# An early exp-table load, and the first pair's half step as one full-height product

## The chip, the cores and the metric

The kernel runs on one core of a Trainium2 chip. The metric is the device time of one execution in microseconds (us), lower is better. Several executions were timed; the median is given with the lowest and the highest. One further execution was taken with the hardware profiler, and its trace is what the views below are read from. The core has five engines with instruction queues of their own: TensorE (PE in the profile, with its weight loads as PEld), VectorE (DVE), ScalarE (ACT), GpSimd (POOL) and SyncE (SP), which here only issues DMAs. A small q behind a name (SPq) is the engine's sequencer.

## The reference

Attention of 8 batches with 12 heads, 448 positions and head size 64, whose softmax has one more term in its denominator; the result, laid out as 3584 tokens of 768, goes through two dense layers with Mish between them.

```python
scores = scale * np.matmul(q, k.transpose(0, 1, 3, 2))
m = np.max(scores, axis=-1, keepdims=True)
e = np.exp(scores - m)
attn = e / (np.sum(e, axis=-1, keepdims=True) + np.exp(-m) + 1e-09)
x = np.matmul(attn, v)              # laid out as (3584, 768)
h = x @ w_in                        # 768 -> 2048
g = h * np.tanh(np.log1p(np.exp(h)))
out = g @ w_out                     # 2048 -> 768
```

## The kernel before, in words

**Pairs, units, batches.** The work goes by pairs of heads: 48 pairs, six to a batch. Three pairs make a unit, two units a batch. The first batch's six pairs run in a head loop (units 0 and 1, L533). From unit 2 on the main loop (L560) runs one unit after the other up to 17. Units 2 to 15 have attention work, and in each of them the dense layers of earlier batches run beside it. Times of a unit in this text count from its exps.

**One unit** has two halves. The first is twelve steps of attention (L571), four for each pair: `exps(idx)` on ScalarE, then a piece of the second dense layer as filler on TensorE (`chunk`, L452 to 464, line L457 in the profile), then `scores_ahead` (L230), which issues the scores of up to three steps ahead. The filler's share of each step is set by `weight` (L495): the first step counts 5.2, the other steps of the first two pairs and the first of the third count 1.0, and the last three 0.4. The second half is eight blocks of the first dense layer with Mish behind each (`mm1_mish`, L384; products L391, Mish L397). Beside them stand the denominators and normalising of the unit's pairs (L303 to 333; the third pair is normalised by GpSimd, L324), the transposes of e through DMA from the SP queue (L330), and the transposes of the next unit's q and k on TensorE (`transpose_pair`, L187), each followed by its copies out of PSUM (`evac_qk`, L195 to 226). At the very end of the half, the scores of the next unit's first three steps are issued (L626; in unit 2 two of them a little earlier, L624).

**Scores, maxima, exps.** Three score tiles of two PSUM banks each go round (L72). A step's scores are written to one of them, VectorE takes the negated row maxima of both banks in one instruction (L278), and ScalarE makes an exp with a running sum of each bank (L291; the sum is read out by an ACTIVATION_READ_ACCUMULATOR). When both exps of a step are done, its tile is free for the step three on. A pair of heads has 896 rows of scores, that is seven blocks of 128, so its last step (s = 3) has one block and uses one bank. The other bank serves as the accumulator of a pair's A·V of the unit before (`av_pair` through `av_with`, L251; products L367, copied out at L376). These A·V products are issued ahead of the last step's scores and so wait for that tile.

**Two layouts of q.** In the second and third pair of a unit from pair 12 on (`is_diag`, L99), q stands in blocks of [head 0 rows | head 1 rows] with zeros in the other head's 64 partitions. One product over all 128 partitions then gives 64 rows of each head (L257). In the first pair of a unit q is plain. Its first three steps take two products of 64 partitions each (L263, L266), and its last half step takes the last 64 rows of head 0 and the first 64 rows of head 1 by two products of 64 partitions and 64 columns (L271, L274).

**Exp and Mish** use different tables of ScalarE. When the function changes, the build puts a table load ahead of the first instruction that needs it. The load ahead of a unit's first exp takes over one or two of that exp's waits. Each unit thus has a load for Mish (shown at L397) and one for exp (shown at L291).

Of the kernel before, what the change touches and what calls it, by code (L numbers as in the profile page):

```python
# [9 lines left out]
FP32 = mybir.dt.float32  # L10
BF16 = mybir.dt.bfloat16
AF = mybir.ActivationFunctionType
# [7 lines left out]
def kernel(  # L20
# [9 lines left out]
    nc = tc.nc  # L30

    B, H, S, D = q.shape
# [10 lines left out]
    N_UNITS = B * UNITS_PER_B  # L43
# [9 lines left out]
    def pool(name, bufs, space=None):  # L53
        if space is None:
            return ctx.enter_context(tc.tile_pool(name=name, bufs=bufs))
        return ctx.enter_context(tc.tile_pool(name=name, bufs=bufs, space=space))

    PS = bass.MemoryType.PSUM
    singles = pool("singles", 1)
# [17 lines left out]

    ident = singles.tile([128, 128], BF16)
    make_identity(nc, ident)
    w_in_sb = singles.tile([128, DM_T, d_ff], BF16)  # L80
    w_out_sb = singles.tile([128, FF_T, d_model], BF16)

# [11 lines left out]
    DIAG_FROM = 2 * HP  # L94
# [3 lines left out]

    def is_diag(p):  # L99
        return p >= DIAG_FROM and p % UNIT_PAIRS > 0  # L100

    loaded, casted, qkT, att, xT, gT, o_sbs, stats = {}, {}, {}, {}, {}, {}, {}, {}
    av_with, mids = {}, {}
# [91 lines left out]
    def evac_qk(p, act=False):  # L195
        if p >= N_PAIRS:
            return
        (q_ps, k_ps), own = qkT[p]
        mo_free.extend(own)
        qd = q_diag[p % 3]  # L200
        kT = qk_pool.tile([128, S], BF16, tag="kT", name="kT")
        if not is_diag(p):
            qT = qd.rearrange("d i h r -> d (i h r)")[:, 0:S]
            qkT[p] = (qT, kT)
            if act:
                nc.scalar.mul(qT, q_ps[:, 0:S], SCALE)
            else:
                nc.vector.tensor_scalar(
                    out=qT, in0=q_ps[:, 0:S], scalar1=SCALE, scalar2=None, op0=ALU.mult
                )  # L210
        else:
            qkT[p] = (qd, kT)
            if p < DIAG_FROM + 3:
                nc.vector.memset(qd[0:64, :, 1, :], 0.0)
                nc.vector.memset(qd[64:128, :, 0, :], 0.0)
            for h in range(2):
                rows = slice(64 * h, 64 * h + 64)
                nc.vector.tensor_scalar(  # L218
                    out=qd[rows, :, h, :],
                    in0=q_ps[rows, 0:S].rearrange("d (i r) -> d i r", i=QB),  # L220
                    scalar1=SCALE, scalar2=None, op0=ALU.mult,
                )
        if p == 0 or own and not act:
            nc.vector.tensor_copy(out=kT, in_=k_ps[:, 0:S])
        else:
            nc.scalar.copy(kT, k_ps[:, 0:S])
# [10 lines left out]
    def scores(idx):  # L237

        p, s = divmod(idx, STEPS)
        if s == 0:  # L240
            if p < HP or p % UNIT_PAIRS == 0:
                for nm in ("negm", "sums", "expm", "den", "rden"):
                    stats[nm] = st_pool.tile([128, UNIT_PAIRS, NTILE], FP32, tag=nm, name=nm)
            at = 0 if p < HP else p % UNIT_PAIRS
            att[p] = {nm: t[:, at, :] for nm, t in stats.items()}
            att[p].update(en=en_bufs[p % N_EN], whole=dict(stats))
        st = att[p]
        qT, kT = qkT[p]
        kA, kB = kT[0:64, :], kT[64:128, :]
        sc = sc_tiles[idx % len(sc_tiles)]  # L250
        if s == STEPS - 1 and p in av_with:  # L251
            av_pair(av_with.pop(p), bank=sc[:, 1, :])
        if is_diag(p):
            cols = tuple(range(2 * s, min(2 * s + 2, NTILE)))
            negm = st["negm"][:, cols[0] : cols[-1] + 1]
            for bk, i in enumerate(cols):
                nc.tensor.matmul(  # L257
                    sc[:, bk, 0:S], lhsT=qT[:, i].rearrange("d h r -> d (h r)"), rhs=kT,
                    start=True, stop=True,
                )  # L260
        elif s < 3:
            qa, qb = 128 * s, 64 + 128 * s
            nc.tensor.matmul(  # L263
                sc[:, 0, 0:S], lhsT=qT[0:64, qa : qa + 128], rhs=kA, start=True, stop=True
            )
            nc.tensor.matmul(  # L266
                sc[:, 1, 0:S], lhsT=qT[64:128, qb : qb + 128], rhs=kB, start=True, stop=True
            )
            cols, negm = (s, 4 + s), st["negm"][:, s : s + 5 : 4]
        else:  # L270
            nc.tensor.matmul(  # L271
                sc[0:64, 0, 0:S], lhsT=qT[0:64, 384:S], rhs=kA, start=True, stop=True
            )
            nc.tensor.matmul(  # L274
                sc[64:128, 0, 0:S], lhsT=qT[64:128, 0:64], rhs=kB, start=True, stop=True
            )
            cols, negm = (3,), st["negm"][:, 3:4]
        nc.vector.tensor_reduce(  # L278
            out=negm, in_=sc[:, 0 : len(cols), 0:S], axis=AX.X, op=ALU.max, negate=True
        )  # L280
        st["sc", s] = (sc, cols)
# [278 lines left out]
    for u in range(UNITS_PER_B, N_UNITS + 2 * UNITS_PER_B):  # L560
        attn = u < N_UNITS
        filler = deque()
        for part in plan.get(u, []):
            filler.extend(mm2_part(*part))
        total, done, acc = sum(w for _, w in filler), 0, 0.0
        p0 = u * UNIT_PAIRS
        if attn and u >= first_mm2:
            av_with.update({p0 + i: p0 + i - UNIT_PAIRS for i in range(UNIT_PAIRS)})
        end = min((u + 1) * UNIT_PAIRS, N_PAIRS) * STEPS

        for n in range(steps):  # L571
            pi, s = divmod(n, STEPS)
            p, idx = p0 + pi, p0 * STEPS + n
            late_tp = u == UNITS_PER_B and n == STEPS
            if late_tp:
                transpose_pair(p0 + 2)
            exps(idx)
            if late_tp:
                evac_qk(p0 + 2)
            if u == UNITS_PER_B + 1:  # L580
                for part in TURN_AT[1].get(n, []):
                    turn_on_pe(*part)
            flush_late()
            acc += weight[n]
            want = int(total * acc / sum(weight) + 1e-6)
            while done < want:
                fn, w = filler.popleft()
                fn()
                done += w
            scores_ahead(end)  # L590
            if n in LOAD_AT:
                load_pair(p0 + LOAD_AT.index(n) + LEAD)
                cast_pair(p0 + LOAD_AT.index(n) + LEAD - 1)
            if u - UNITS_PER_B < len(AV_AT):
                early = AV_AT[u - UNITS_PER_B]
                if n in early:
                    av_pair(early[n])
                if u == UNITS_PER_B:
                    for part in TURN_AT[0].get(n, []):
                        turn_on_pe(*part)  # L600
            elif u == N_UNITS and n in LAST_AV_AT:
                av_pair(p0 - UNIT_PAIRS + LAST_AV_AT.index(n))
            if u - UNITS_PER_B < len(W_AT):
                load_w(W_AT[u - UNITS_PER_B].get(n, 0))
        assert done == total

        moe = u < N_UNITS + UNITS_PER_B
        b, w = (u - UNITS_PER_B) // UNITS_PER_B, u % UNITS_PER_B
        nxt = p0 + UNIT_PAIRS
        todo = sorted(range(p0, nxt), key=lambda p: p in BY_PE)  # L610
        for f in range(FF_U):
            if moe:
                mm1_mish(b, w * FF_U + f)
            if u == UNITS_PER_B and f in (2, 6):
                load_w(1)
            if not attn:
                continue
            if f == 0:
                denominators(att[p0]["whole"])
                normalise(todo[0], dma=todo[0] not in BY_PE)  # L620
            if f in (1, 3, 5):
                transpose_pair(nxt + f // 2, bank=f // 2 % 2)
                evac_qk(nxt + f // 2)
            if nxt < DIAG_FROM and f in (4, 6):  # L624
                scores_ahead(nxt * STEPS + f // 2 - 1)
            if f == FF_U - 1:  # L626
                scores_ahead(min(nxt * STEPS + 3, N_PAIRS * STEPS))
            if f == 3:
                normalise(todo[1], dma=todo[1] not in BY_PE)
            if f == 4:  # L630
                normalise(todo[2], dma=todo[2] not in BY_PE, on_pool=True)
        if moe and w == UNITS_PER_B - 1:
            gather_mid(b)
    flush_late()
# [31 lines left out]
```

## Time and profile before

| | us |
|---|---|
| median of 3 runs | 483.12 (482.86 to 483.24) |
| the profiled execution | 483.85 |
| its span in the trace | 482.0 |
| TensorE busy | 446.8 |
| ScalarE busy | 348.8 |
| VectorE busy | 339.1 |
| GpSimd busy | 175.2 |

The span is the time from the first to the last instruction of the program in the trace; the execution's own time has 1.85 us around it. Busy time is counted once where instructions of an engine overlap. The chain of waits follows the work that ended last back to the start: at each step to what released it, or to the instruction before it on its engine. Rows of the timeline give start, duration, engine, line, operation, output and inputs, count, and in brackets how long the engine was idle before and what ended that. Ends of matmuls are modelled, and consecutive products overlap by a little.

### The profile page before, as it was taken

What the parts mean: (1) busy time and instruction counts of PE and PEld (TensorE: products, weight loads), DVE (VectorE), ACT (ScalarE), POOL (GpSimd) and SP (SyncE); (2) the same over time, 40 slices, a digit from 0 to 9 for tenths busy, and PEclk for the clock granted to TensorE, in tenths of its full rate; (3) what the DMA queues carried; (4) which work ended last, traced back from release to release, by engine and by line L of the source; (5) the groups of instructions that cost most, each with busy time, mean ns of one, the idle gap of its engine ahead of it and who ended that gap; (6) DMA issues with size and microseconds to landing.
All of it is one profiled execution on the core that took longest, in us unless ns stands there. A gap on an engine that the chain in (4) does not pass through costs nothing.

```text
span 482.0 us, 8971 instructions
## 1 busy us (share of the span) xinstructions
PE 446.8 (93%) x3076; PEld 250.2 (52%) x3076; DVE 339.1 (70%) x679; ACT 348.8 (72%) x906; POOL 175.2 (36%) x290
## 2 busy tenths in 40 slices
PE   4566888898999999999999999999999999999997
PEld 2233544454555555555555555555555555556565
DVE  4877987978777886878687878788687868420021
ACT  5978787878797888979697979888797979502300
POOL 4866808345414234343434232333434330300000
PEclk9997698899999999999999999999999999999999
DMA  8999959999999999798989989897989595770103
GB/s 224 211 230 230 229 87 242 166 190 248 195 210 250 230 215 215 212 204 237 198 242 185 227 167 232 200 225 201 197 233 212 147 179 136 136 159 19 48 25 107
DMA packets 202381, 90.37 MB, mean 188 GB/s; under 512 B 159072, under 2 KB 198880, under 8 KB 202336
## 3 DMA queue, kind: packets, MB, share of 16 engines
q1 hardware_dynamic: 194848, 83.51, 78.8%
q0 software_dynamic: 7488, 6.29, 8.9%
q8 instruction: 24, 0.39, 0.3%
q14 instruction: 21, 0.17, 0.1%
HBM read 45.61 MB, written 11.01 MB: 117 GB/s over the span
## 4 chain that ended last, share of the span: by engine, by line
PE 68%; ACT 17%; DVE 10%; DMA 2%; issue 2%; SPq 0%; ACTq 0%; DVEq 0%
PE mo L391 25%; PE mo L457 18%; ACT en L291 12%; DVE negm L278 8%; PE sc L367 6%; PE sc L257 5%; PE sc L391 3%; ACT L291 3%; PE sc L187 3%; PE sc L263 2%; PE mo L341 2%; DMA eT<-en 2%; PE mo L367 1%; PE sc L271 1%; DVE en L326 1%
## 5 line engine op out<-in xcount | busy, mean ns | idle before, releaser
L291 ACT ACTIVATE en<-sc,negm 128x448 bf16<-128x448 f32 x336 | 209.8, 638 | 21.2 <-DVE negm L278 11.6
L278 DVE TENSOR_REDUCE negm<-sc 128x2 f32<-128x896 f32 x192 | 180.8, 969 | 60.2 <-PE sc L266 26.2
L457 PE MATMUL mo<-w_out_sb,gT 128*128 128x384 bf16 (+1 forms) x912 | 142.4, 301 | 0.0
L391 PE MATMUL mo<-xT,w_in_sb 128*128 128x448 bf16 x672 | 137.3, 352 | 1.3 <-DVE xT L376 1.2
L324 POOL TENSOR_SCALAR en<-en,rden 128x448 bf16<-128x448 bf16 x122 | 76.5, 646 | 127.7 <-DVE rden L316 104.0
L397 ACT ACTIVATE gT<-mo 128x448 bf16<-128x448 f32 x112 | 61.4, 548 | 67.7 <-PE mo L391 67.5
L457 PEld LDWEIGHTS <-gT 128*128 128x128 bf16 x912 | 83.1, 98 | 49.5 <-issue 8.1
L391 PEld LDWEIGHTS <-w_in_sb 128*128 128x128 bf16 x768 | 72.9, 98 | 64.0 <-issue 2.8
L291 ACT ACTIVATION_READ_ACCUMULATOR en<-sc,negm 128x1 f32 x336 | 69.5, 207 | 0.0
L169 POOL CAST q_bf<-q_f 112x512 bf16<-112x512 f32 x47 | 29.0, 618 | 99.7 <-DMA q_f<-in_q_dram 99.5
L326 DVE TENSOR_SCALAR en<-en,rden 128x448 bf16<-128x448 bf16 x214 | 58.3, 345 | 0.9
L444 DVE COPY o_sb<-mo 128x384 f32<-128x384 f32 (+1 forms) x65 | 32.2, 495 | 35.1 <-PE mo L457 34.8
L257 PE MATMUL sc<-kT,qd 128*128 128x448 bf16 x168 | 47.7, 354 | 0.2 <-ACT en L291 0.2
L263 PE MATMUL sc<-kT,qd 64*128 64x448 bf16 x72 | 25.9, 421 | 12.6 <-ACT en L291 11.9
L367 PE MATMUL sc<-eT,v_bf 112*64 112x448 bf16 x288 | 34.1, 356 | 3.6 <-ACT en L291 1.9
L367 PEld LDWEIGHTS <-v_bf 112*64 112x64 bf16 x384 | 22.0, 113 | 24.4 <-issue 14.0
L156 POOL CAST v_bf<-v_f 112x512 bf16<-112x512 f32 x48 | 29.5, 615 | 7.3 <-DMA v_f<-in_v_dram 6.1
L170 POOL CAST k_bf<-k_f 112x512 bf16<-112x512 f32 x47 | 28.9, 615 | 8.5 <-DMA k_f<-in_k_dram 8.0
L218 DVE TENSOR_SCALAR qd<-sc 64x448 bf16<-64x448 bf16 x48 | 18.7, 389 | 11.4 <-PE sc L187 10.7
L266 PE MATMUL sc<-kT,qd 64*128 64x448 bf16 x72 | 26.2, 426 | 0.0
L257 PEld LDWEIGHTS <-qd 128*128 128x128 bf16 x168 | 16.3, 97 | 17.9 <-issue 9.2
L457 PE MATMUL mo<-w_out_sb,mid 128*128 128x384 bf16 x128 | 24.9, 326 | 0.0
(50 smaller groups left out, 340.0 us busy)
## 6 DMA issues: line engine op xcount, KB each, us to landing
q_f<-in_q_dram SPq DMA_DIRECT2D x48, 224.0 KB, 4.9
k_f<-in_k_dram SPq DMA_DIRECT2D x48, 224.0 KB, 5.3
v_f<-in_v_dram SPq DMA_DIRECT2D x48, 224.0 KB, 5.6
w_in_sb<-in_moe_w_in_dram POOLq DMA_DIRECT2D x12, 256.0 KB, 5.8
w_out_sb<-in_moe_w_out_dram POOLq DMA_DIRECT2D x8, 384.0 KB, 7.8
out_dram<-o_sb SPq DMA_DIRECT2D x7, 336.0 KB, 4.0
out_dram<-o_sb SPq DMA_DIRECT2D x8, 288.0 KB, 4.3
out_dram<-o_sb SPq DMA_DIRECT2D x8, 240.0 KB, 3.1
```

The source lines that it names most:

```text
L156: nc.gpsimd.tensor_copy(out=casted[p][2], in_=loaded.pop(p)[2])
L257: nc.tensor.matmul(sc[:, bk, 0:S], lhsT=qT[:, i].rearrange("d h r -> d (h r)"), rhs=kT, start=True, stop=True,)
L263: nc.tensor.matmul(sc[:, 0, 0:S], lhsT=qT[0:64, qa : qa + 128], rhs=kA, start=True, stop=True)
L278: nc.vector.tensor_reduce(out=negm, in_=sc[:, 0 : len(cols), 0:S], axis=AX.X, op=ALU.max, negate=True)
L291: nc.scalar.activation(out=st["en"][:, :, c, 0:SP_], in_=sc[:, bk, 0:S].rearrange("q (j c) -> q j c", j=NT), func=AF.Exp, bias=st["negm"][ ...
L324: nc.gpsimd.tensor_scalar(scalar2=1.0, op0=ALU.mult, op1=ALU.mult, **args)
L326: nc.vector.tensor_scalar(scalar2=None, op0=ALU.mult, **args)
L367: nc.tensor.matmul(av[h * 64 : (h + 1) * 64, 0:S], lhsT=v_bf[:, h, j * D : (j + 1) * D], rhs=e_h, start=(j == 0), stop=(j == NT - 1),)
L391: nc.tensor.matmul(h_ps[:, 0:S], lhsT=w_in_sb[:, dm, ff * 128 : (ff + 1) * 128], rhs=xT[b][:, dm, :], start=(dm == 0), stop=(dm == DM_T - 1),)
L397: nc.scalar.activation(out=gT[b][:, ff, :], in_=h_ps[:, 0:S], func=AF.Mish)
L444: nc.vector.tensor_copy(out=o_sb[:, cols], in_=st["o"][:, 0:n_cols])
L457: nc.tensor.matmul(st["o"][:, 0:n_cols], lhsT=src[:, ff, c0 : c0 + 128], rhs=w_out_sb[:, ff, cols], start=(ff == 0), stop=(ff == FF_T - 1),)
```

## The change

Two edits, which share no data.

At the end of each unit that has attention and is followed by another such unit (units 2 to 14, thirteen times), ScalarE gets an exp of one column of zeros into a tile that nobody reads. It stands right behind the last Mish. As built, the table load stands in front of this exp, with no wait; the unit's first real exp keeps all its waits and has no load ahead of it. The zeros are written once, by VectorE, at the start.

For the first pair of each unit from pair 12 on, GpSimd copies the two 64x64 pieces of q that the half step needs into a tile `q_rest` of two blocks, cleared once at the start, so that head 0's piece stands in partitions 0 to 63 of the first block and head 1's in partitions 64 to 127 of the second. The half step is then one product over 128 partitions with 128 columns. VectorE's writing of the next first pair's q waits for these copies, and the half step's weight load waits for them too.

```diff
     ident = singles.tile([128, 128], BF16)
     make_identity(nc, ident)
+    zero = singles.tile([128, 1], FP32)
+    one = singles.tile([128, 1], FP32)
+    nc.vector.memset(zero, 0.0)
...
+    q_rest = singles.tile([128, 2, 64], BF16)
+    nc.gpsimd.memset(q_rest, 0.0)
...
                 nc.vector.tensor_scalar(
                     out=qT, in0=q_ps[:, 0:S], scalar1=SCALE, scalar2=None, op0=ALU.mult
                 )
+            if p >= DIAG_FROM:
+                nc.gpsimd.tensor_copy(out=q_rest[0:64, 0, :], in_=qT[0:64, 384:S])
+                nc.gpsimd.tensor_copy(out=q_rest[64:128, 1, :], in_=qT[64:128, 0:64])
...
             cols, negm = (s, 4 + s), st["negm"][:, s : s + 5 : 4]
+        elif p >= DIAG_FROM:
+            nc.tensor.matmul(
+                sc[:, 0, 0:S], lhsT=q_rest.rearrange("d h r -> d (h r)"), rhs=kT,
+                start=True, stop=True,
+            )
+            cols, negm = (3,), st["negm"][:, 3:4]
         else:
...
                 normalise(todo[2], dma=todo[2] not in BY_PE, on_pool=True)
+        if attn and u + 1 < N_UNITS:
+
+            nc.scalar.activation(out=one, in_=zero, func=AF.Exp)
         if moe and w == UNITS_PER_B - 1:
             gather_mid(b)
```

## The prediction

> **What bounds the kernel now.** I read the page first, then the chain of waits, then the timeline of one unit whole, and last the places where units differ.
>
> ```profile
> PE 446.8 (93%) x3076; PEld 250.2 (52%) x3076; DVE 339.1 (70%) x679; ACT 348.8 (72%) x906; POOL 175.2 (36%) x290
> PE 68%; ACT 17%; DVE 10%; DMA 2%; issue 2%; SPq 0%; ACTq 0%; DVEq 0%
> L291 ACT ACT_TABLE_LOAD x13 | 16.7, 1283 | 10.1 <-DVE negm L278 10.1
> 157.20 1.28 ACT L291
> ...
> 394.32 1.28 ACT L291
> ```
>
> TensorE is busy 93% of the span, yet a third of the chain lies elsewhere. The groups by line have 13 loads of exp's table, 1.283 us each, ahead of which ScalarE idles 10.1 us for VectorE's maxima. The chain of waits runs through such a load at every unit boundary; from 157.20 (unit 6) to 394.32 (unit 15) there are ten, (394.32 - 157.20) / 9 = 26.35 us apart. So these ten units are copies of each other, and one timeline serves for all. Here are the rows of the unit whose exps begin at 237.60 (columns: start, duration, engine, line, tiles, count, idle before and its releaser).
>
> ```profile
> 234.84 0.55 ACT L397 ACTIVATE gT<-mo 128x448 bf16<-128x448 f32 x1 [0.59 <-PE mo L391]
> 235.14 3.09 DVE L278 TENSOR_REDUCE negm<-sc 128x2 f32<-128x896 f32 x3 [1.90 <-PE sc L266]
> 235.41 3.44 PE L457 MATMUL mo<-w_out_sb,gT 128*128 128x192 bf16 x28
> 236.30 1.28 ACT L291 ACT_TABLE_LOAD   x1 [0.92 <-DVE negm L278]
> 237.60 0.64 ACT L291 ACTIVATE en<-sc,negm 128x448 bf16<-128x448 f32 x1
> ...
> 238.74 0.20 ACT L291 ACTIVATION_READ_ACCUMULATOR en<-sc,negm 128x1 f32 x1
> ...
> 238.99 0.95 PE L367 MATMUL sc<-eT,v_bf 112*64 112x448 bf16 x8
> ...
> 239.87 0.37 PE L271 MATMUL sc<-kT,qd 64*64 64x448 bf16 x1
> 239.87 0.37 PE L274 MATMUL sc<-kT,qd 64*64 64x448 bf16 x1
> ...
> 240.18 0.82 PE L457 MATMUL mo<-w_out_sb,gT 128*128 128x384 bf16 x4
> ...
> 240.35 0.62 DVE L278 TENSOR_REDUCE negm<-sc 128x1 f32<-128x448 f32 x1 [1.86 <-PE sc L274]
> ```
>
> The last Mish ends at 234.84 + 0.55 = 235.39. ScalarE then idles 0.92 us, since the table load carries the wait for the first maxima, loads for 1.28 us, and starts exps at 237.60. The first score tile is free when the second exp's sum is read, at 238.74 + 0.20 = 238.94, and the first A·V (L367), which borrows half of that tile, starts at 238.99. Was TensorE late for it anyway? Compare it with the second and third A·V of the unit:
>
> ```profile
> 242.61 0.63 ACT L291 ACTIVATE en<-sc,negm 128x448 bf16<-128x448 f32 x1 [0.28 <-DVE negm L278]
> 243.27 0.81 PE L457 MATMUL mo<-w_out_sb,gT 128*128 128x384 bf16 x4
> ...
> 244.01 0.95 PE L367 MATMUL sc<-eT,v_bf 112*64 112x448 bf16 x8
> ...
> 244.89 0.36 PE L257 MATMUL sc<-kT,qd 128*128 128x448 bf16 x1
> ...
> 245.09 0.81 PE L457 MATMUL mo<-w_out_sb,gT 128*128 128x384 bf16 x4
> ...
> 248.18 0.81 PE L457 MATMUL mo<-w_out_sb,gT 128*128 128x384 bf16 x4
> 248.94 0.95 PE L367 MATMUL sc<-eT,v_bf 112*64 112x448 bf16 x8
> ```
>
> The products ahead of those end at 243.27 + 0.81 = 244.08 and 248.99 by the model, and A·V starts 0.07 and 0.05 us before that end: consecutive products overlap. The 28 products ahead of the first A·V end at 235.41 + 3.44 = 238.85, so without ScalarE it would start at 238.78. The true stall is **0.21 us** a unit. The early filler (weight 5.2 in the plan) already covers the rest of the table load.
>
> **The change, part by part.** *The early load.* As built, a load without waits now stands behind the last Mish, then the 128x1 exp, then the first real exp, which keeps all its waits and needs no load. A dummy of that size is not in the trace; the nearest rows:
>
> ```profile
> L301 ACT ACTIVATE expm<-negm 128x21 f32<-128x21 f32 x14 | 3.0, 214 | 0.0
> L298 ACT ACTIVATE expm<-negm 128x7 f32<-128x7 f32 x6 | 1.5, 247 | 0.0
> ```
>
> I take 0.21 us (bounds 0.10, half the smaller, and 0.25). Load from 235.39, dummy from 236.67, first exp at 236.88 at best; the maxima that it waits for were out at 236.30, when the old load could start. That is 237.60 - 236.88 = 0.72 us earlier, so the tile is free at 238.22, ahead of the 238.78 at which TensorE arrives. Of 0.72 us, 0.21 reaches TensorE; what is late next is TensorE's own filler, and ScalarE will wait for the fourth maxima instead. The dummy's 0.21 us is covered by the other 0.51.
>
> The Trainium skill ("ScalarE: Activation LUTs", What ACT_TABLE_LOAD costs) puts about 1283 ns on the load and a drain of about 1380 ns beside it for each switch. The load agrees with the row; the drain does not show: exp starts at 237.60, 1.30 us after the load's start at 236.30.
>
> *The half step as one product.* The two quarter-array products take 240.18 - 239.87 = 0.31 us until the next product starts; the third pair step of full height (L257, alone) takes 245.09 - 244.89 = 0.20. TensorE gains 0.11 us a unit. Whether it keeps that, the loop through VectorE and ScalarE decides: from this half step to the next A·V it is 244.01 - 239.87 = 4.14 us in the first pair and 248.94 - 244.89 = 4.05 in the second, where the form already is the new one. The first pair then does what the second does, so I take 4.14 - 4.05 = **0.09 us** (bounds 0 and 0.11).
>
> *GpSimd's two copies* of 64x64 wait for VectorE's q of the first pair. Their price lies between the smallest and the nearest work that I find there:
>
> ```profile
> masks.py:197 POOL MEMSET ident<- 128x128 bf16 x1 | 0.2, 205 | 0.3 <-POOLq L650 0.3
> L169 POOL CAST q_bf<-q_f 112x512 bf16<-112x512 f32 x47 | 29.0, 618 | 99.7 <-DMA q_f<-in_q_dram 99.5
> ...
> 228.29 0.38 DVE L208 TENSOR_SCALAR qd<-sc 128x448 bf16<-128x448 bf16 x1
> ...
> 232.59 4.33 POOL L324 TENSOR_SCALAR en<-en,rden 128x448 bf16<-128x448 bf16 x7 [5.82 <-DVE rden L316]
> ```
>
> 0.1 to 0.62 us each, nearer to 0.2, from 228.67 on, inside GpSimd's idle 5.82 us, with the product that reads them 11 us later. Behind them in GpSimd's queue stands only the normalising at 232.59, whose own release comes from VectorE. Cost nothing; if that cover went, at most 1.2 us of a normalising whose transpose is needed 12 us later. VectorE's next q waits for copies a unit old: nothing. The two clears at the start (GpSimd 0.2 us, VectorE about 0.2) stand ahead of casts that wait for the first loads: nothing. No DMA is moved, and SP's queue keeps its order.
>
> *Where the dummy is not covered.* Units 3 and 4 differ, and so does unit 5:
>
> ```profile
> 76.78 1.28 ACT L291 ACT_TABLE_LOAD   x1
> 79.47 0.35 PE L271 MATMUL sc<-kT,qd 64*64 64x448 bf16 x1 [2.07 <-ACT en L291]
> 103.34 1.28 ACT L291 ACT_TABLE_LOAD   x1
> 106.03 0.95 PE L367 MATMUL sc<-eT,v_bf 112*64 112x448 bf16 x8 [0.23 <-ACT en L291]
> 129.96 7.94 DMA eT<-en
> 138.04 0.95 PE L367 MATMUL sc<-eT,v_bf 112*64 112x448 bf16 x8 [0.22 <-DMA eT<-en]
> ```
>
> At 76.78 and 103.34 the load has no idle time before it: it already stands right behind Mish, with nothing left to wait for. There the dummy only adds 0.21 us, and TensorE waits for ScalarE in both (2.07, 0.23). That is +0.42 us. In unit 5 the second A·V waits for a transpose that lands at 129.96 + 7.94 = 137.90. What this unit gains ahead of it (0.30) is lost there, and the 0.42 passes on only as far as the transpose is itself later: net between 0 and +0.42, and I take +0.3, since that transpose hangs on normalising that follows the delayed exps.
>
> *Sum.* Ten units (6 to 15) x (0.21 + 0.09) = -3.0 us, units 3 to 5 +0.3: **-2.7 us**. The profiled execution took 483.85 us (482.0 of span and 1.85 around it), so 481.15 in its terms; the median of the runs shown is 0.73 lower, 483.12, which gives **480.4 us**.
>
> **The rivals.** (1) *Only the load counts*: the loop through VectorE paces the first pair whatever TensorE saves; for it speaks that ScalarE waits for maxima there (0.28 us at 242.61), against it the 4.14 beside 4.05. Ten x 0.21 less 0.3: 481.3 us. (2) *The early load buys nothing*: the first A·V is held by something else that ends near 238.9. Against it, the tile is free at 238.94 and A·V starts 0.05 us later. Ten x 0.09 less 0.3: 482.5 us. (3) *More than forecast*: the transpose in unit 5 does not hold, the dummy is near 0.1 us. Eleven units x (0.21 + 0.11) less 0.2: 479.8; were unit 4 to gain like the others and nothing lost, twelve x 0.32 = 3.9 gives 479.2. (4) *Slower*: the dummy stalls ScalarE, between Mish and the first exp, by as much again as a load (1.28 us), as if the change added a switch and took none away. It decides from 0.72 us on, the lead worked out above. Exp would start at 236.88 + 1.28 = 238.16, 0.56 late: ten units x (0.56 - 0.09) = 4.7, and 1.28 + 0.21 each in units 3 and 4, some 8 us, 491 us. Against it: in the trace exp follows its load in 0.02 us. With the Trainium skill's drain of 1.38 us at this place instead (the page above) an estimate is 492 us; the row shows none. (5) *The change doesn't do what it says*: the load stays with the real exp. As built it does not, so this has no share of its own beyond (2).
>
> **How the numbers follow.** Forecast 0.62, (1) 0.14, (2) 0.14, (3) 0.05, (4) 0.05. A measurement of this kernel can tell some 0.2%, 0.97 us, from no change, so the line is at 482.15. Forecast, (1) and (3) are faster: 0.81. (2) lies within: 0.14. (4) is slower: 0.05. The range takes in the forecast's unknown terms (part two 0 to 0.11, unit 5), (1) and (3): 479.2 to 482.2, with (2) and (4) outside, 0.19.
>
> **What would show it.** After the change, the 13 loads should stand without idle time ahead of them, the first exp of a late unit some 1.5 us behind Mish's end instead of 2.2, and the first A·V about 0.07 us before its products' modelled end. ScalarE's idle time ahead of exps should grow by about 0.5 us a unit. The next product should start 0.20 us behind the half step, and late boundaries should lie 26.05 us apart. In units 3 and 4 the half step or A·V should come 0.2 us later behind Mish. Wrong would be: boundaries still 26.3 us apart, a first A·V that still waits for ScalarE, or the loss of units 3 to 5 above 1 us.

## The result, and the profile after

The changed kernel takes 479.94 us (median of 6 runs, 479.34 to 480.30). The kernel before, timed beside it, took 483.37 us (6 runs, 482.86 to 484.47). The ratio is 0.9925, with a 95% interval of 0.9912 to 0.9938: 3.4 us faster, by the interval between 3.0 and 4.3 us. The forecast was 480.4 us, a gain of 2.7, which is less than the interval's lower end.

The page of the changed kernel and its groups by line (lines below L103 have moved; the short exp and its load are at L649, the half step at L280, GpSimd's copies at L218 and L219):

```profile
PE 443.1 (93%) x3064; PEld 248.6 (52%) x3064; DVE 339.1 (71%) x680; ACT 350.0 (73%) x919; POOL 181.1 (38%) x315
PE 76%; ACT 10%; DVE 9%; issue 2%; DMA 1%; POOL 0%; SPq 0%; DVEq 0%; ACTq 0%; POOLq 0%
L649 ACT ACT_TABLE_LOAD x13 | 16.7, 1283 | 0.2
L649 ACT ACTIVATE one<-zero 128x1 f32<-128x1 f32 x13 | 2.6, 203 | 0.1
L218 POOL COPY q_rest<-qd 64x64 bf16<-64x64 bf16 x12 | 2.8, 231 | 36.5 <-DVE qd L214 36.5
L219 POOL COPY q_rest<-qd 64x64 bf16<-64x64 bf16 x12 | 2.8, 236 | 0.7
```

There are still 13 loads of 1.283 us; what went is the idle time ahead of them, 10.1 us to 0.2. TensorE's share of the chain rose from 68% to 76%, ScalarE's fell from 17% to 10%. The timeline of the same unit as before:

```profile
233.10 0.54 ACT L412 ACTIVATE gT<-mo 128x448 bf16<-128x448 f32 x1 [0.59 <-PE mo L406]
233.66 1.28 ACT L649 ACT_TABLE_LOAD   x1
233.67 3.44 PE L472 MATMUL mo<-w_out_sb,gT 128*128 128x192 bf16 x28
234.95 0.20 ACT L649 ACTIVATE one<-zero 128x1 f32<-128x1 f32 x1
235.06 0.62 ACT L306 ACTIVATE en<-sc,negm 128x448 bf16<-128x448 f32 x1
...
236.19 0.20 ACT L306 ACTIVATION_READ_ACCUMULATOR en<-sc,negm 128x1 f32 x1
...
237.04 0.95 PE L382 MATMUL sc<-eT,v_bf 112*64 112x448 bf16 x8
...
237.92 0.36 PE L280 MATMUL sc<-kT,q_rest 128*128 128x448 bf16 x1
238.12 0.81 PE L472 MATMUL mo<-w_out_sb,gT 128*128 128x384 bf16 x4
...
239.64 0.64 ACT L306 ACTIVATE en<-sc,negm 128x448 bf16<-128x448 f32 x1 [0.79 <-DVE xT L391]
...
241.97 0.95 PE L382 MATMUL sc<-eT,v_bf 112*64 112x448 bf16 x8
...
246.90 0.95 PE L382 MATMUL sc<-eT,v_bf 112*64 112x448 bf16 x8
```

Mish ends at 233.10 + 0.54 = 233.64. The first exp follows 1.42 us behind it, at 235.06 (2.21 before), and the first tile is free at 236.39. The first A·V starts at 237.04, 0.07 us before the modelled end of its 28 products (233.67 + 3.44 = 237.11): TensorE comes last now. That is 3.40 us behind Mish instead of 3.60. The half step is followed by the next product in 238.12 - 237.92 = 0.20 us instead of 0.31, and the first and second A·V are 4.93 us apart instead of 5.02, as the second and third are. ScalarE pays its lead back: 0.79 us idle at 239.64. Over the whole kernel its idle time ahead of real exps rose from 21.2 to 26.4 us (the pages' first group, L291 before and L306 after), about the 0.5 us for each of ten units that was forecast.

So where did 4 us of span go? The chain of waits of the two kernels gives the first dense product of units 2 and 6, and the table loads give the late units.

```profile
64.83 1.41 PE mo L391 x6
...
171.75 1.14 PE mo L391 x6
```

```profile
63.40 1.41 PE mo L406 x6
...
170.63 1.14 PE mo L406 x6
```

```profile
155.50 1.28 ACT L649 ACT_TABLE_LOAD   x1
...
389.81 1.28 ACT L649 ACT_TABLE_LOAD   x1
```

Up to unit 2's dense half, 1.43 us less; from there to unit 6's, 107.23 instead of 106.92, 0.31 us more; from unit 6's load to unit 15's, 234.31 instead of 237.12, **2.81 us less**, 26.03 us a unit instead of 26.35. The late units do what was forecast, 26.03 us against 26.05. (Unit 6 is in both of the last two stretches, so they can't simply be added.) The 1.43 us of the head are a surprise, since the change puts nothing there but two clears. The experiments take up three questions: whether the late gain is the sum of two independent parts, where ScalarE's lead ends, and whether the head's gain is the change's.

### The profile page after: what moved, and what is told of

Read it like the earlier page. It is cut to its first block, busy times and chain, and to the rows that moved or that the text cites. A ratio compares the mean times of both kernels' runs of the same rounds, so it can differ in the third digit from the quotient of the medians.

```text
span 478.0 us, 8924 instructions
## 1 busy us (share of the span) xinstructions
PE 443.1 (93%) x3064; PEld 248.6 (52%) x3064; DVE 339.1 (71%) x680; ACT 350.0 (73%) x919; POOL 181.1 (38%) x315
## 4 chain that ended last, share of the span: by engine, by line
PE 76%; ACT 10%; DVE 9%; issue 2%; DMA 1%; POOL 0%; SPq 0%; DVEq 0%; ACTq 0%; POOLq 0%
PE mo L472 26%; PE mo L406 25%; ACT en L306 9%; PE sc L382 6%; DVE negm L293 6%; PE sc L266 5%; PE sc L406 4%; PE sc L193 3%; PE sc L272 2%; PE mo L356 1%; PE mo L382 1%; DVE en L341 1%; PE sc L280 1%; DVE eT L360 1%; DMA k_f<-in_k_dram 1%
## 5 line engine op out<-in xcount | busy, mean ns | idle before, releaser
L306 ACT ACTIVATE en<-sc,negm 128x448 bf16<-128x448 f32 x336 | 209.6, 637 | 26.4 <-DVE xT L391 10.4
L472 PEld LDWEIGHTS <-gT 128*128 128x128 bf16 x912 | 84.1, 98 | 48.2 <-issue 5.7
L306 ACT ACTIVATION_READ_ACCUMULATOR en<-sc,negm 128x1 f32 x336 | 69.3, 206 | 0.0
L272 PE MATMUL sc<-kT,qd 64*128 64x448 bf16 x72 | 25.1, 411 | 12.7 <-ACT en L306 11.1
L382 PEld LDWEIGHTS <-v_bf 112*64 112x64 bf16 x384 | 21.0, 112 | 22.8 <-issue 13.6
L275 PE MATMUL sc<-kT,qd 64*128 64x448 bf16 x72 | 25.4, 415 | 0.0
```

What stands on the lines that cost most here:

```text
L272: nc.tensor.matmul(sc[:, 0, 0:S], lhsT=qT[0:64, qa : qa + 128], rhs=kA, start=True, stop=True)
L306: nc.scalar.activation(out=st["en"][:, :, c, 0:SP_], in_=sc[:, bk, 0:S].rearrange("q (j c) -> q j c", j=NT), func=AF.Exp, bias=st["negm"][ ...
L382: nc.tensor.matmul(av[h * 64 : (h + 1) * 64, 0:S], lhsT=v_bf[:, h, j * D : (j + 1) * D], rhs=e_h, start=(j == 0), stop=(j == NT - 1),)
L472: nc.tensor.matmul(st["o"][:, 0:n_cols], lhsT=src[:, ff, c0 : c0 + 128], rhs=w_out_sb[:, ff, cols], start=(ff == 0), stop=(ff == FF_T - 1),)
```

## The experiments

Each kernel here computes the whole reference and is the kernel before or the changed kernel with the edit given. Each was timed with runs of the kernel before beside it, and its ratio is to those: their median was 482.90 us for the first four below, 483.04 for seven short exps and for the filler in all units, 483.37 for the other two. "Late" is the time from unit 6's table load to unit 15's, nine units: 237.12 us before, 234.31 after.

**The early load alone.** The changed kernel without `q_rest`, its clear, its copies and its branch in `scores`.

> The early load alone, the half step as before. Theory (TensorE paces the late units, the load takes 0.21 us of stall out of each, and costs one short exp, net 0.11 us, in units 3 and 4): first A.V 3.40 us behind the last Mish instead of 3.60 in units 6 to 15; first to second A.V stays at 5.02; late period 26.3 -> 26.1; ten x 0.21, about 0.3 more in unit 5, less 0.2: about -2.2 us against the kernel before (ratio 0.9954). Rival (the half step's form carries most of the gain): less than -1.2 us, period still 26.3. Rival (a faster head from the new clears or the shifted tiles makes about 1 us of the change's gain): -3.2 us, with the first dense product of unit 2 at 63.4 instead of 64.8.

Measured: 481.37 us (12 runs), ratio 0.9970 (0.9957 to 0.9984), 1.5 us faster than before.

```profile
155.26 1.28 ACT L637 ACT_TABLE_LOAD   x1
...
158.64 0.95 PE L370 MATMUL sc<-eT,v_bf 112*64 112x448 bf16 x8
...
390.80 1.28 ACT L637 ACT_TABLE_LOAD   x1
```

First A·V 158.64 - 155.26 = 3.38 us behind the load, as in the changed kernel (237.04 - 233.66); the pairs stay 5.03 us apart. Late: 235.54, 1.58 us less. The mechanism is as expected, the time 0.7 us short of it. Half of that stands in one place in the trace: in unit 8 the second and third A·V are 5.28 us apart instead of 4.93. There a row maximum starts 0.37 us later behind its product than elsewhere:

```profile
216.72 0.36 PE L260 MATMUL sc<-kT,qd 128*128 128x448 bf16 x1
...
217.55 0.62 DVE L281 TENSOR_REDUCE negm<-sc 128x1 f32<-128x448 f32 x1 [0.62 <-PE sc L260]
```

The same 5.28 at the same place stands in one other kernel (the clears alone, below), and in none that has the copies. Its cause was not tried. Without it the late units would gain 1.58 + 0.35 = 1.93, close to 9 x 0.21 = 1.89.

**The half step alone.** The changed kernel without the short exp and its two tiles.

> The half step as one product alone, the table load where it was. Theory: first A.V still 3.60 us behind Mish; half step to next product 0.20 instead of 0.31; first to second A.V 5.02 -> 4.93, held there by the loop through VectorE and ScalarE; ten x 0.09 = -0.9 us (ratio 0.9981); unit 5 nothing, since its second A.V waits for a transpose. Rival (loop paces the first pair whatever TensorE saves): spacing stays 5.02 and the time is the same, 0 us. Rival (TensorE keeps all): 4.91 and -1.1 us. Rival (faster head): about -2 us.

Measured: 481.70 us (12 runs), ratio 0.9975 (0.9963 to 0.9988), 1.2 us faster.

```profile
155.91 1.28 ACT L303 ACT_TABLE_LOAD   x1 [0.92 <-DVE negm L290]
...
392.14 1.28 ACT L303 ACT_TABLE_LOAD   x1 [0.92 <-DVE negm L290]
```

Late: 236.23, 0.89 us less; ScalarE idles 0.92 us ahead of each late load as before, and the first two A·V are 4.93 us apart. So it is worth 0.10 us a unit by itself (0.89 / 9). The first rival (0) fell. The period lies midway between the theory's 0.09 and the second rival's 0.11 (TensorE keeps all) and doesn't decide between them; that the first two A·V now stand 4.93 us apart, like the second and third, speaks for the theory. The two parts add: with the slow place taken out, 1.93 + 0.89 = 2.82 against 2.81 measured together.

**No early load in units 3 and 4.**

```diff
-        if attn and u + 1 < N_UNITS:
+        if attn and 4 <= u and u + 1 < N_UNITS:
```

> Both edits, but the early load only at the ends of units 4 to 14, not 2 and 3. Theory (in units 3 and 4 the old load already stood right behind Mish, the short exp only costs there): exp of units 3 and 4 1.31 us behind Mish instead of 1.42, so 0.1 to 0.2 us faster than the changed kernel, about -3.6 us against before (ratio 0.9925), not to be told from the changed kernel by time alone. Rival (the early load helps in units 3 and 4 too): some tenths slower than the changed kernel. Rival (0.5 us lost in each of units 3 and 4 of the changed kernel's profile comes from the short exp): 0.8 us faster than the changed kernel.

Measured: 479.87 us (6 runs), ratio 0.9938 (0.9923 to 0.9953). Exps of units 3 and 4 stand 1.31 us behind Mish, in the changed kernel 1.42. Its median is the changed kernel's within 0.1 us, as expected; against the runs beside it, it is 3.0 us faster, and not the 3.6 expected. Unit 5 shows where the rest goes; the first two A·V of that unit in the changed kernel and in this one:

```profile
132.15 0.95 PE L382 MATMUL sc<-eT,v_bf 112*64 112x448 bf16 x8
...
137.15 0.95 PE L382 MATMUL sc<-eT,v_bf 112*64 112x448 bf16 x8
```

```profile
132.36 0.95 PE L382 MATMUL sc<-eT,v_bf 112*64 112x448 bf16 x8
...
138.21 0.95 PE L382 MATMUL sc<-eT,v_bf 112*64 112x448 bf16 x8 [0.87 <-DMA eT<-en]
```

Here the second A·V waits 0.87 us for its transpose, in the changed kernel it comes without such a wait. Over the profiles the two are between 5.00 and 5.97 us apart where 4.93 would do, 5.31 and 5.32 in the two profiles of before; only with seven short exps, where TensorE comes later, are they at 4.93.

**The clears alone.** The kernel before with the three new tiles and both clears, which nothing reads.

> The kernel before with the new tiles and their two clears at the start, which nothing reads: no early load, no new product. Theory (the head's 1.4 us between the two profiles is TensorE's granted clock, which falls to half in other stretches from run to run, and not the change): same time, ratio 1.000, late period 26.3 us, and the first dense product of unit 2 anywhere between 63 and 65 us. Rival (placement of the tiles or the clears speed the head up): -1 us or more, ratio 0.998, and a first dense product at 63.4.

Measured: 483.75 us (11 runs), ratio 1.0018 (1.0008 to 1.0028): not faster, 0.9 us slower. First dense product at 64.77, and the period is 26.31 us in all late units but two, units 8 and 12, which are longer in the kernel before as well. In the trace, the slow place in unit 8 named above gives 0.35 us of the loss. Another 0.34 stands in unit 5. From Mish to Mish, that is from the end of the last Mish ahead of its exps to the end of the last one ahead of unit 6's, it takes 27.50 us instead of 27.16, with the second A·V 5.54 us behind the first and 0.45 us of wait for its transpose. Why the kernel is slower with tiles that nobody reads was not found.

**The kernel before, once more.**

> The kernel before, unchanged, one more profile. Theory (the head's time hangs on where the granted clock falls to half): first dense product of unit 2 between 63 and 65 us, other than 64.83 by some tenths, with the half-clock stretches elsewhere; late periods 26.30 again, second A.V of unit 5 late by another amount. Rival (the head is fixed for a program): 64.8 again, same stretches.

Measured: one execution, 482.95 us, span 481.1; first dense product of unit 2 at 64.20. The clock rows of the pages of before, before again, and after:

```profile
PEclk9997698899999999999999999999999999999999
```

```profile
PEclk9999698999999999999999999999999999999999
```

```profile
PEclk9998798899999999999999999999999999999999
```

Slice 4 (36.1 to 48.2 us in the first) is at 7 in the first profile, at 9 in the second, though the program is the same. There, A·V products of eight matmuls took, in the first profile and in that of the changed kernel:

```profile
39.86 1.71 PE L367 MATMUL mo<-eT,v_bf 112*64 112x448 bf16 x8
```

```profile
39.23 0.95 PE L382 MATMUL mo<-eT,v_bf 112*64 112x448 bf16 x8
```

In the second profile a product of that kind took 0.97 us at 40.02. In the traces the granted clock falls to half in stretches of 3.4 us or multiples of it, at places that differ from run to run: in the head at 39.3 to 42.7 and 46.1 to 56.4 us in the first profile, 46.3 to 56.5 in the second, 44.5 to 54.8 in the changed kernel's. Over eleven profiles of ten kernels whose head does the same work but for the clears, the first dense product of unit 2 came at 63.3 to 64.9 us. The first profile lies at the slow end, that of the changed kernel at the fast end. The 1.43 us are within this spread, and one program alone differs by 0.63 (64.83 and 64.20). That the change has no part in them is likely and not shown. Nor is it shown that the clock is the whole cause: behind 10.2 us at half clock that product came at 63.40 in the changed kernel and at 64.91 with a first filler weight of 4.4 (below).

**Seven short exps, then three.** The changed kernel with

```diff
-            nc.scalar.activation(out=one, in_=zero, func=AF.Exp)
+            for _ in range(7):
+                nc.scalar.activation(out=one, in_=zero, func=AF.Exp)
```

> Seven short exps. Theory: lag 2.6 to 2.9, beyond the knee at 2.01; first A.V = lag + 1.39, about 4.0 to 4.3 us behind Mish, so each of the ten late units takes 0.6 to 0.9 us more than in the changed kernel, 26.6 to 26.9, and units 3 and 4 lose 1.3 each: +9 to +12 us against the changed kernel, some 2 per cent slower than before. It places the point from which the short exp costs. Rival (TensorE's other work takes up the delay later in the unit): periods stay under 26.3.

Measured: 490.69 us (4 runs), ratio 1.0163 (1.0146 to 1.0180), 10.8 us above the changed kernel's median.

```profile
157.19 0.54 ACT L412 ACTIVATE gT<-mo 128x448 bf16<-128x448 f32 x1 [0.59 <-PE mo L406]
157.75 1.28 ACT L649 ACT_TABLE_LOAD   x1
159.05 1.61 ACT L649 ACTIVATE one<-zero 128x1 f32<-128x1 f32 x7
160.56 0.62 ACT L306 ACTIVATE en<-sc,negm 128x448 bf16<-128x448 f32 x1
...
161.94 0.95 PE L382 MATMUL sc<-eT,v_bf 112*64 112x448 bf16 x8 [0.74 <-ACT en L306]
...
399.33 1.28 ACT L649 ACT_TABLE_LOAD   x1
```

Exp now stands 160.56 - 157.73 = 2.83 us behind Mish, and A·V 1.38 us behind exp, waiting 0.74 for ScalarE. Late: 399.33 - 157.75 = 241.58, 26.84 a unit, 0.81 more than the changed kernel.

With `range(3)` in place of `range(7)`:

> The changed kernel with three short exps behind each Mish. Seven of them gave a lag of 2.83 us and a first A.V at 4.20, so 0.235 us for each further one and 1.37 from exp to A.V. Theory (a lead that nothing uses): lag 1.42 + 2 x 0.235 = 1.89, under the knee at 3.40 - 1.37 = 2.03; first A.V stays at 3.40 and the late period at 26.00; only units 3 and 4 lose 0.47 each: +0.5 to +0.9 us against the changed kernel, about -2.2 us against before (ratio 0.9955). Rival (all of ScalarE's earliness is used): late period 26.47, slower than before by 2 us.

Measured: 481.28 us (7 runs), ratio 0.9959 (0.9944 to 0.9974), 2.1 us faster than before as expected, and 1.3 us above the changed kernel's median where 0.5 to 0.9 was expected.

```profile
155.94 1.28 ACT L649 ACT_TABLE_LOAD   x1
157.23 0.67 ACT L649 ACTIVATE one<-zero 128x1 f32<-128x1 f32 x3
157.81 0.62 ACT L306 ACTIVATE en<-sc,negm 128x448 bf16<-128x448 f32 x1
...
159.31 0.95 PE L382 MATMUL sc<-eT,v_bf 112*64 112x448 bf16 x8
...
390.24 1.28 ACT L649 ACT_TABLE_LOAD   x1
```

Exp is 0.47 us later than with one short exp (1.89 behind Mish), and the late units do not notice: 234.30 against 234.31. Between them the two runs show the knee: ScalarE may come 0.47 us later for nothing, and 1.41 us later costs 0.81 a unit, so it lies near 1.41 - 0.81 = 0.60 us.

**Less filler ahead of the first A·V.**

```diff
-    weight = [5.2] + [1.0] * (steps - STEPS) + [0.4] * (STEPS - 1)
+    weight = [4.4] + [1.0] * (steps - STEPS) + [0.4] * (STEPS - 1)
```

> The changed kernel with a first filler weight of 4.4 instead of 5.2: less filler ahead of the first A.V, more behind it, since the first tile is now free about 0.6 us before TensorE comes. Theory (TensorE has no idle time left there, so its filler only moves): first A.V about 0.3 us earlier behind Mish, but the pairs behind it longer by as much, late period 26.0 within 0.1, same time as the changed kernel. Rival (the lead of ScalarE is worth something once TensorE comes earlier): period 25.8 or less, 2 us faster than the changed kernel.

Measured: 480.80 us (4 runs), ratio 0.9952 (0.9937 to 0.9967). In the late units the first A·V comes 3.06 us behind Mish, the second and third are 5.23 apart instead of 4.93 (5.08 in units 8 and 12), and the period is 25.98. For the most part the filler only moved; units 8 and 12, which took 26.16 in the changed kernel, take 25.98 as well. Unit 5 took 27.95 us from Mish to Mish instead of 26.74: its first A·V waited 0.47 us for a transpose, its second 1.00 us, which the trace puts down to a row maximum.

**What the runs point to.** The early load from unit 4's end on, with 4.4 in units 6 to 15 alone:

```diff
-            acc += weight[n]
-            want = int(total * acc / sum(weight) + 1e-6)
+            by = [4.4] + weight[1:] if 6 <= u < N_UNITS else weight
+            acc += by[n]
+            want = int(total * acc / sum(by) + 1e-6)
```

> Both edits, the early load from unit 4's end on, and a first filler weight of 4.4 in units 6 to 15 alone. From the profile with 4.4 in all units: late periods 25.98 instead of 26.00, and 25.98 instead of 26.16 in the two units whose third A.V waited; the loss in unit 5 (27.57 instead of 26.08) and in unit 16 (21.92 instead of 21.66) should stay out. Theory: 0.5 us from the late units, 0.1 to 0.2 from units 3 and 4, so about 0.6 us faster than the changed kernel, ratio to before 0.9915. Rival (the unit 5 transpose eats what is gained ahead of it): the same as the changed kernel.

Measured: 479.18 us (5 runs, 478.56 to 479.61), ratio 0.9913 (0.9898 to 0.9929). Its median is 0.8 us below the changed kernel's, the intervals of the two overlap. In its trace the late units take 25.98 us each, also the two that took 26.16 in the changed kernel: over nine units 0.51 us less.

## Why the prediction was right, and where it was off

- **A stall of 0.21 us at the first A·V, 0.21 of ScalarE's 0.72 us of lead reaching TensorE.** Right: 3.60 to 3.40 us behind Mish in every late unit, and about 9 x 0.21 with the load alone. The lead came out at 2.21 - 1.42 = 0.79, because the short exp costs less than its 0.20 us: the next exp starts 0.11 us behind its start. The unused part, forecast at 0.51, is near 0.60 by the runs with three and seven.
- **0.09 us from the half step, not 0.11.** Right in kind: the first pair now does what the second does, 4.93 us. In size it came out between the two, 0.10 (0.89 over nine units alone). Beside the early load it is not lost, as the sum of the two parts shows.
- **GpSimd's copies hidden.** Right, 0.23 us each; no product waits for them.
- **Units 3 to 5 at +0.3 us.** This term is where the sum was off. The short exp was put at 0.21 us in units 3 and 4 and costs 0.11 behind Mish; unit 4 took 25.88 us from Mish to Mish instead of 25.80. Unit 3 took 27.54 instead of 26.56, which would be 1.0 us lost, but the granted clock was at half from 88.9 to 92.3 us of this profile: sixteen A·V products took 2.91 us from 88.57 on, in the kernel with the early load alone 1.70 from 89.29 on, and there unit 3, with the same short exp, took 26.55. So that loss goes with the clock's stretch and not with the short exp.

  In unit 5 the forecast was that the transpose holds the second A·V and the gain ahead of it is lost. In this profile it was not lost, 26.74 us instead of 27.16, with the second A·V 5.00 us behind the first; in others the transpose held it, up to 0.87 us. Taken together the three units lost 0.98 + 0.08 - 0.42 = 0.64 us, which agrees with the chain: 0.31 us longer between the dense halves of units 2 and 6, with a gain of 0.3 in unit 6 itself. Without the clock's stretch it would be a gain of some 0.3 us and not a loss. But unit 5 may have been free of its wait because unit 3 came late, so what the change does to units 3 to 5 without that stretch stays open.
- **The sum, 2.7 us.** The ten late units were put at -3.0; nine of them measured -2.81, which is 3.1 for ten. The measured gain of 3.4 us (3.0 to 4.3) thus leaves 0.3 us of gain, by the interval between a loss of 0.1 and a gain of 1.2, for everything outside the late units, where the forecast had a loss of 0.3. The two parts alone give 1.5 and 1.2, 2.7 together, and the first of them has a slow place of 0.35 us that the changed kernel lacks; the kernel without early loads in units 3 and 4 gives 3.0. No run shows to which step the 0.3 us belong. The head's share in the two profiles is within what it differs by from run to run.
- **Rivals.** That only the load counts fell with the half step alone; that the load buys nothing fell with the load alone. The third rival, 479.8 us, is nearer to the measured 479.94 than the forecast's 480.4. Of its three conditions the short exp at 0.1 us came true (0.11), the transpose in unit 5 did not hold in the one profile of the changed kernel, and the half step stayed under 0.11. The slower rival, a stall behind the short exp, needs 0.72 us: seven short exps make such a stall, and the kernel became 1.6% slower. The Trainium skill ("ScalarE: Activation LUTs", What ACT_TABLE_LOAD costs) puts a drain of about 1380 ns on each switch beside the load. Behind the load it would have made that stall here. The trace shows none: the load starts 0.02 us behind Mish's end, it ends at 233.66 + 1.28 = 234.94, and the short exp starts at 234.95.

## What to carry to other kernels

In this kernel the table load stood behind what its first user waits for; a one-column activation that waits for nothing, put where the last use of the old table ends, takes the load out from behind that wait. It pays only where the load had idle time ahead of it, and only as much as the other engine's own work leaves open, so measure that engine's stall at the point of meeting (0.21 us here) and not the idle time removed (0.92). A full-height product with zeros in it can be cheaper than two quarter products side by side: here, ahead of a full-height product, 0.20 us against 0.31; other neighbours were not tried. Whether the pair of engines behind it can follow is read from the same place in a pair that already has the form.

## What was not expected of the hardware

The granted clock's half-speed stretches stood at other places in two profiles of one program, and the head ended at 64.83 and 64.20 us. Over all eleven profiles its end moved by up to 1.6 us, half as much as the whole change is worth. One such stretch, at 88.9 us in the changed kernel's profile, went with a loss of about 1 us in unit 3. In two kernels a VectorE instruction in unit 8 started 0.37 us late at the same place, in eight others it did not.
